# Segment recalls as sixteen packed products behind a block's values, from a dense memory

## Chip, cores and metric

The kernel runs on one core of one Trainium2 chip. The metric is the device time of a run in microseconds (us), as the median of several runs. Most runs of this kernel agree within 0.3%. All arithmetic that decides the output is done on fp32 data; the large products are made of split operands (a high part in the format fp32r and a remainder).

## The reference

One token block goes through a layer norm, and then through two branches whose outputs are added to the input: an attention with a running memory, and a gated feed-forward network. Cut to what matters:

```python
xn = layernorm(x)                        # S = 2048 tokens, D = 448
# attention, H = 16 heads of Dh = 28; 4 segments of L = 512 tokens
phi = lambda t: where(t > 0, t + 1, exp(t))
M, z = 0, 0                              # per head: 28 x 28, and 28
for s in range(4):
    qs, ks, vs = q[s], k[s], v[s]
    a_dot = softmax(qs @ ks.T * scale + causal_mask) @ vs
    num = phi(qs) @ M                    # the recall of a segment
    den = phi(qs) @ z + 1e-6
    o[s] = g * num / den + (1 - g) * a_dot      # g = sigmoid(beta), per head
    M = M + phi(ks).T @ vs               # the update of the memory
    z = z + phi(ks).sum(over tokens)
out = x + o @ wo + (sigmoid(xn @ w_gate) * (xn @ w_up)) @ w_down
```

The first segment's memory is empty, so only three segments have a recall.

## The kernel before

A block is a segment of 512 tokens; there are four (b = 0 to 3). The program has a front and a second phase.

*The front* goes block by block. The order of PE, ACT and DVE in it is the order in which the code is written (`tc.manual_schedule`); SP and POOL get their instructions by a scheduler. For each block, `values(b, t)` multiplies four groups of 128 tokens by the value weights (11 passes of 448 columns each, L335) and puts them into `vst`, where each head takes 32 columns: 28 values, and ones from column 28 on. Then `keys_queries(b, c)` makes seven products of 128 rows (11 passes of 512 columns, L355; c = 0 to 3 hold the keys, 3 to 6 the queries). Each is split on ACT and DVE into two parts that are stored to DRAM (`qd`, L363), and phi of it is made in a tile `e` (ACT: relu and exp; DVE: L365). Phi of queries is stored to `fd` (L368). Phi of keys is turned by four transposes (`key_rows`, L375) and copied by ACT into `kn`, tokens by keys. Between them PE turns the next block's normalised tokens (`turn`, L95; DVE finishes them at L102 and L103), and DVE normalises them (`normalise`, L320).

*The memory* is kept in four tiles `mst` of 112 rows (four heads of 28) and 128 columns (the same four heads' 32 columns of values). `update(b, i)` multiplies `kn` and `vst` for four heads at once, which also gives the products of different heads; a mask `heads` takes these away on DVE (L386, or L389 and L390).

*The recall* of four heads, `recall(b, i, phi)`, is one product of 112 rows with 512 tokens (L401) into a bank "m" or "pd". DVE evaluates it with five instructions: a transpose of 32 by 32 squares into `ts` (L402), three in `weigh` that divide by the ones' column and multiply by the head's gate (L132, L133, L136), and a transpose back into `tb` (L404), which POOL's queue stores to `od` (L405). The recalls of block b - 1 stand in block b for b = 2 and 3: three of them between the values, the fourth behind the first key product. Their four tiles of phi queries (`phi`, 112 rows each, L394) share the five buffers of the tag "e".

*The last block* (b = 3) makes the keys and queries that its own recalls need in another order, c = 3, 4, 5, 6, 0, 1, 2, and begins with the feed-forward network: `next(ffn)` takes one step of the generator `gated`, whose gate products `pgu` (L248) stand between the key products, and whose weights are loaded by SP (`load_up` into `raw`, `load_down` into `rawd`) and split by ACT and DVE (`ready_up`, `ready_down`, L85 and L86). The recalls of block 3 itself stand behind the last two key products and then between gate products. `FILLS` says how many steps of the network come ahead of each of the last two.

*The second phase* runs the network, the attention of 16 units and the output projection against each other; PE's and SP's order there is that of the code. The first scores `st` (L612) stand right behind the gate products at its start.

PSUM's eight banks are shared by tags: two "p", two "s", one "m", two "gu", one "pd". A tile asked of a tag waits until the older one in that bank has been read. In SBUF, `two_k` is a ring of two tiles of 512 columns, which the network's `sg` uses (ACT's tanh L256 writes it, DVE reads it in L257 and L260), and `four_k` one of four pairs (`qk`, `hh`).

```python
def two_k(name):
    return mid.tile([P, L], F32, name=name, tag="2k", bufs=2)
sg = two_k("sg")
A.activation(sg, pgu[0], AF.Tanh, scale=0.5)
V.scalar_tensor_tensor(sg, sg, 1.0, pgu[1], op0=ALU.add, op1=ALU.mult)
```

## Time and profile before

| what | us |
|---|---|
| median of the runs (3; 691.22 to 691.61) | 691.52 |
| the profiled execution's own time | 691.24 |
| its span, first to last instruction | 689.6 |
| the span, by stage: blocks 0 and 1 | 0 to 78 |
| block 2 (the first with recalls) | 78 to 115 |
| block 3, with the network's first steps | 115 to 157 |
| second phase | 157 to 689.6 |

TensorE's granted clock is 1.00 in every stage. PE (TensorE) does the matmuls and transposes, PEld its weight loads, which overlap them; DVE is VectorE, ACT is ScalarE, POOL is GpSimd and SP issues most DMAs. A line such as L401 is a line of the program printed above. PE's records are of 3594 matmuls, of which some are passes of one product: a product of fp32 data is made in two passes, so a recall's row shows "x2".

### The profile page before, as it was taken

To read this page: it belongs to the slowest core of one execution; us is meant where nothing else is said; L and a number is where in the kernel's file an instruction comes from. 1 tells how busy PE (TensorE), PEld (TensorE's weight loads), DVE (VectorE), ACT (ScalarE), POOL (GpSimd) and SP (SyncE) were. 2 spreads that over 40 slices of the span, in tenths; PEclk is the share of its full clock that TensorE was granted. 3 is DMA by queue.
4 is the path that set the end of the run, shared out by engine and by line. 5 is a ranking of instruction groups with operands and counts; after the bars stand their busy time and mean duration, and the time that the engine had idled before them with its cause. 6 is when DMAs were issued, how large, how long until landed. Compare 5 with 4: busy or idle time off the path is not lost.

```text
span 689.6 us, 10445 instructions
## 1 busy us (share of the span) xinstructions
PE 682.4 (99%) x3594; PEld 565.6 (82%) x3594; DVE 569.7 (83%) x994; ACT 342.6 (50%) x563; POOL 146.0 (21%) x349
## 2 busy tenths in 40 slices
PE   8999999999999999999999999999999999999997
PEld 7898888778878787788878878787787878878897
DVE  6765795767889898989898989998889889889863
ACT  5837555343455555544555446455544555446220
POOL 4500020101222122221222223222232322222000
PEclk9999999999999999999999999999999999999999
DMA  7446566696243233333233342324342432333342
GB/s 266 183 146 240 194 224 235 255 331 161 77 102 95 61 86 86 81 112 102 56 71 103 70 123 56 101 55 116 81 114 56 96 72 71 86 95 80 91 155 106
DMA packets 45797, 84.37 MB, mean 122 GB/s; under 512 B 6321, under 2 KB 20401, under 8 KB 45233
## 3 DMA queue, kind: packets, MB, share of 16 engines
q1 hardware_dynamic: 42736, 76.37, 35.9%
q0 software_dynamic: 3008, 7.34, 4.9%
q8 instruction: 28, 0.46, 0.3%
q14 instruction: 25, 0.20, 0.1%
HBM read 51.05 MB, written 32.64 MB: 121 GB/s over the span
## 4 chain that ended last, share of the span: by engine, by line
PE 77%; DVE 10%; issue 7%; POOL 3%; ACT 1%; DMA 1%; SPq 0%; POOLq 0%; ACTq 0%
PE pgu L248 30%; PE pd L173 14%; PE pp L355 10%; PE po L771 5%; PE pv L335 5%; PE st L612 4%; PE pa L687 4%; DVE mx L629 2%; POOL w L627 2%; PE pmm L383 2%; PE n L401 1%; DVE acc L176 1%; DVE w L666 1%; DMA acc<-in_x 1%; PE pt L95 1%
## 5 line engine op out<-in xcount | busy, mean ns | idle before, releaser
L248 PE MATMUL pgu<-xs,wgu 128*128 128x512 f32 x1232 | 316.8, 395 | 0.0
L248 PEld LDWEIGHTS pgu<-xs,wgu 128*128 128x128 f32 x1232 | 226.6, 188 | 45.0 <-issue 3.2
L173 PE MATMUL pd<-wdn,hh 128*128 128x448 f32 x672 | 161.8, 367 | 0.0
L667 ACT ACTIVATE w<-w 128x1024 f32<-128x1024 f32 (+1 forms) x96 | 87.1, 915 | 96.5 <-DVE w L666 95.8
L173 PEld LDWEIGHTS pd<-wdn,hh 128*128 128x128 f32 x672 | 123.0, 188 | 14.5 <-issue 0.6
L627 POOL TENSOR_SCALAR_AFFINE_SELECT w<-w 128x256 f32<-128x256 f32 (+1 forms) x160 | 79.1, 496 | 251.5 <-ACT w L616 216.3
L666 DVE TENSOR_TENSOR w<-w,mb 128x1024 f32<-128x1024 f32 (+1 forms) x96 | 99.7, 1050 | 0.2
L616 ACT ACTIVATE w<-st 128x512 f32<-128x512 f32 x128 | 74.8, 588 | 41.3 <-PE st L612 41.2
L629 DVE TRANSPOSE_TENSOR_REDUCE mx<-w 128x32 f32<-128x1024 f32 x64 | 79.1, 1235 | 12.9 <-POOL w L627 12.8
L355 PE MATMUL pp<-xs,wqk 128*128 128x512 f32 x308 | 77.7, 401 | 0.0
L176 DVE TENSOR_TENSOR acc<-pd,acc 128x448 f32<-128x448 f32 x112 | 67.4, 602 | 2.0 <-PE pd L173 2.0
L355 PEld LDWEIGHTS pp<-xs,wqk 128*128 128x128 f32 x308 | 56.8, 188 | 13.4 <-issue 2.4
L612 PE MATMUL st<-qk 84*128 84x128 f32 (+3 forms) x256 | 64.1, 311 | 0.4 <-ACT w L616 0.3
L259 ACT ACTIVATE hh<-sg 128x512 fp32r<-128x512 f32 x56 | 35.1, 626 | 47.3 <-DVE sg L257 37.3
L612 PEld LDWEIGHTS st<-qk 84*128 84x128 f32 x256 | 48.4, 189 | 9.3 <-ACT w L616 1.9
L256 ACT ACTIVATE sg<-pgu 128x512 f32<-128x512 f32 x56 | 33.2, 593 | 33.4 <-PE pgu L248 32.9
L656 DVE STREAM_TRANSPOSE mb<-top 128x1024 f32<-128x1024 f32 x32 | 39.8, 1243 | 10.3 <-POOL top L653 10.1
L362 DVE TENSOR_TENSOR qk<-pp,qk 128x512 fp32r<-128x512 f32 x28 | 19.3, 688 | 29.8 <-ACT e L360 23.7
L257 DVE SCALAR_TENSOR_TENSOR sg<-sg,pgu 128x512 f32<-128x512 f32 x56 | 37.4, 668 | 4.3 <-PE pgu L248 4.3
L260 DVE SCALAR_TENSOR_TENSOR hh<-sg,hh 128x512 fp32r<-128x512 f32 x56 | 38.4, 685 | 2.4 <-ACT hh L259 2.2
L335 PE MATMUL pv<-wv,xs 128*128 128x448 f32 x176 | 39.8, 376 | 0.2
L687 PE MATMUL pa<-w,vv 128*32 128x128 f32 (+3 forms) x512 | 39.6, 436 | 0.1
(100 smaller groups left out, 637.3 us busy)
## 6 DMA issues: line engine op xcount, KB each, us to landing
qk<-qd SPq DMA_DIRECT2D x192, 112.0 KB
qd<-qk SPq DMA_DIRECT2D x28, 512.0 KB
raw<-in_w_ffn SPq DMA_DIRECT2D x14, 512.0 KB
vd<-vst SPq DMA_DIRECT2D x4, 1024.0 KB
vv<-vd SPq DMA_DIRECT2D x16, 256.0 KB
od<-w POOLq DMA_DIRECT2D x16, 256.0 KB, 3.8
sums<-od SPq DMA_DIRECT2D x32, 128.0 KB
out<-acc SPq DMA_DIRECT2D x16, 224.0 KB
```

The lines of the kernel that those rows point to most:

```text
L173: T.matmul(pd[:, :D], l, r, start=n == 0, stop=n == len(mms) - 1)
L176: V.tensor_add(acc[b][:, t, :], pd[:, :D], acc[b][:, t, :])
L248: T.matmul(dst, wgu[f][:, w, side * P:(side + 1) * P], xs[b][:, a, :], start=n == 0, stop=n == len(TERMS) - 1)
L335: T.matmul(pv[:, :D], xs[b][:, a, t * P:(t + 1) * P], wv[w], start=n == 0, stop=n == len(TERMS) - 1)
L355: T.matmul(pp, wqk[c][:, w, :], xs[b][:, a, :], start=n == 0, stop=n == len(TERMS) - 1)
L612: T.matmul(st[:, at:at + L - kb * P], self.qk[:KS, 1, h, kb * P:(kb + 1) * P], self.qk[:KS, 0, h, kb * P:], start=True, stop=True)
L616: A.activation(w, st, AF.Copy)
L627: G.affine_select(d, d, pattern=pattern, base=0, channel_multiplier=-1, compare_op=ALU.is_ge, fill=MASK)
L629: V.tensor_reduce(mx[:, 16 * (n - 1):16 * (n + 1)], w3[:, n // 2, :2 * L].rearrange("p (b n) -> p b n", n=32), axis=mybir.AxisListType.X, ...
L666: V.tensor_sub(w, w, m)
L667: A.activation(w, w, AF.Exp, scale=SCALE)
L687: T.matmul(pa[32 * j:32 * j + 32, kb * P:], self.vv[:, kb, 32 * j:32 * j + 32], self.pairs[j // 2].block(j % 2, kb), start=kb == 0, stop=k ...
```

## The change

Memory becomes dense: one tile `mst` of 128 rows and 128 columns, whose square of 32 rows (i) and 32 columns (j) is head 4j + i. The update's product has values for weights and keys as moving columns, each head's 28 keys and four further columns (`by_head`; behind `kn`'s last key stand zeros). DVE transposes the result into `dm`, one store for each bank of four heads, and after the fourth takes the squares of each row group from it with one copy or addition each: four for a block. The mask is gone.

A segment's recalls are sixteen products of 28 rows and 32 columns, each at its own position of the array (`tile_position=(32i, 32j)`). Row group i writes bank i; its four column groups fill that bank's 128 rows. They stand in one group: behind all of a block's values for blocks 2 and 3, and for the last block's own behind the last key product and the gate products after it. The evaluation, `recalled`, is apart: the first right behind the products, the other three behind the first, second and third key product, and for the last block's own recalls all four in a row. `ts` now comes from the ring `two_k`, as does `dm`. The gates are also kept by the new order of heads (four more small loads of `beta`). Phi of queries is one tile with a buffer of its own, loaded by four DMAs of 28 rows; `e` has four buffers instead of five. The stores to `od` take every fourth head.

```diff
...
 FRONT = {mybir.EngineType.PE, mybir.EngineType.Activation, mybir.EngineType.DVE}
 FILLS = (2, 2)
 WARM = 10
+EB = 4
+TB = 2
...
         return ps.tile([P, L], F32, name=name, tag=tag, bufs=banks[tag])
-    gate = keep.tile([P, NG], F32, name="gate")
+    gate = keep.tile([P, NG + HG], F32, name="gate")
     gate_n = keep.tile([P, NG], F32, name="gate_n")
...
     with tc.tile_pool(name="front", bufs=2) as sb, tc.manual_schedule(engines=FRONT):
-        heads = sb.tile([P, P], F32, name="heads", bufs=1)
...
-        mst = [[sb.tile([GW, P], F32, name=f"mst{n}_{i}", bufs=1) for i in range(NG)] for n in range(2)]
+        mst = [sb.tile([P, P], F32, name=f"mst{n}", bufs=1) for n in range(2)]
...
             if (c < 4 and b < NB - 1) or (c > 2 and b > 0):
-                e = sb.tile([P, L], F32, name="e", tag="e", bufs=5)
+                e = sb.tile([P, L], F32, name="e", tag="e", bufs=EB)
                 A.activation(e, pp, AF.Relu, scale=-1.0)
                 A.activation(e, e, AF.Exp, scale=-1.0)
             V.tensor_sub(qk[:, 1, :], pp, qk[:, 0, :].bitcast(F32))
...
                     nc.sync.dma_start(fd[b][lo:(c + 1) * P - D], e[D + lo - c * P:])
             return e
+        def by_head(a):
+
+            return bass.AP(a.tensor, a.offset, [list(a.ap[0]), [DH, HG], [1, 32]])
+
         def key_rows(c, e):
             pk = bank("pk", ("m", "pd")[c % 2])
...
             n = min(P, D - c * P)
             A.activation(kn[:, :, c * P:c * P + n], pk.rearrange("p (t n) -> p t n", t=NT)[:, :, :n], AF.Copy)
-        def update(b, i):
-
-            pmm = bank("pmm", ("pd", "m")[i % 2])
+        turned = {}
+
+        def update(b, j):
+
+            if j == 0:
+                turned[b] = two_k("dm").rearrange("p (j n) -> p j n", n=P)
+            dm = turned[b]
+            pmm = bank("pmm", ("pd", "m")[j % 2])
             for t in range(NT):
-                T.matmul(pmm[:GW, :P], kn[:, t, i * GW:(i + 1) * GW], vst[:, t, HG * i:HG * (i + 1), :],
-                         start=t == 0, stop=t == NT - 1)
-            if b == 0:
-                V.tensor_mul(mst[1][i], pmm[:GW, :P], heads[:GW])
-            else:
-                dm = sb.tile([GW, P], F32, name="dm")
-                V.tensor_mul(dm, pmm[:GW, :P], heads[:GW])
-                V.tensor_add(mst[(b + 1) % 2][i], mst[b % 2][i], dm)
-
-        def phi_queries(b, i):
-            phi = sb.tile([GW, L], F32, name="phi", tag="e", bufs=5)
-            nc.sync.dma_start(phi, fd[b][i * GW:(i + 1) * GW])
-            return phi
-
-        def recall(b, i, phi):
-            ts = sb.tile([P, L], F32, name="ts", bufs=1)
-            tb = sb.tile([P, L], F32, name="tb", bufs=2)
-            n2 = bank("n2", ("m", "pd")[i % 2])
-            T.matmul(n2, mst[b % 2][i], phi, start=True, stop=True)
-            V.transpose(ts, n2)
-            weigh(sb, ts, gate[:, i:i + 1], MEM_EPS)
+                keys = by_head(kn[:, t, GW * j:GW * j + HG * 32])
+                T.matmul(pmm[:, :P], vst[:, t, HG * j:HG * (j + 1), :], keys, start=t == 0, stop=t == NT - 1)
+            V.transpose(dm[:, j, :], pmm[:, :P])
+            if j == HG - 1:
+                for i in range(NG):
+                    rows = slice(32 * i, 32 * i + 32)
+                    after, before = (mst[(b + n) % 2][rows, :].rearrange("p (j c) -> p j c", c=32) for n in (1, 0))
+                    if b == 0:
+                        V.tensor_copy(after, dm[rows, :, rows])
+                    else:
+                        V.tensor_add(after, before, dm[rows, :, rows])
+
+        def phi_queries(b, phi):
+            for i in range(HG):
+                nc.sync.dma_start(phi[32 * i:32 * i + DH],
+                                  fd[b].rearrange("(j i d) n -> i d j n", i=HG, d=DH)[i])
+
+        def recall(b, phi, tags):
+
+            n2 = [bank("n2", tag) for tag in tags]
+            for i in range(HG):
+                rows = slice(32 * i, 32 * i + DH)
+                for j in range(NG):
+                    cols = slice(32 * j, 32 * j + 32)
+                    T.matmul(n2[i][cols, :], mst[b % 2][rows, cols], phi[rows, j, :], start=True, stop=True,
+                             tile_position=(32 * i, 32 * j))
+            return n2
+
+        def recalled(b, i, n2):
+            ts = two_k("ts")
+            tb = sb.tile([P, L], F32, name="tb", bufs=TB)
+            V.transpose(ts, n2[i])
+            weigh(sb, ts, gate[:, NG + i:NG + i + 1], MEM_EPS)
             V.transpose(tb, ts)
-            nc.gpsimd.dma_start(od[b][P * i:P * (i + 1)], tb)
+            nc.gpsimd.dma_start(od[b].rearrange("(j i c) n -> i j c n", i=HG, c=32)[i], tb)
...
         with nc.allow_non_contiguous_dma(reason="a strip's heads"):
             for j in range(HG):
-                nc.sync.dma_start(gate[32 * j:32 * j + 32], beta[j::HG].partition_broadcast(32))
+                nc.sync.dma_start(gate[32 * j:32 * j + 32, :NG], beta[j::HG].partition_broadcast(32))
+            for j in range(NG):
+                nc.sync.dma_start(gate[32 * j:32 * j + 32, NG:], beta[HG * j:HG * j + HG].partition_broadcast(32))
...
         split_qk(2)
-        G.memset(heads, 1.0)
-        h3 = heads.rearrange("p (j c) -> p j c", c=32)
-        G.affine_select(h3, h3, pattern=[[-DH, HG], [0, 32]], base=0, channel_multiplier=1,
-                        compare_op=ALU.is_ge, fill=0.0)
-        G.affine_select(h3, h3, pattern=[[DH, HG], [0, 32]], base=DH - 1, channel_multiplier=-1,
-                        compare_op=ALU.is_ge, fill=0.0)
+        G.memset(kn[:, :, D:], 0.0)
         ffn = gated()
         for b in range(NB):
             last = b == NB - 1
-            phi, xn = {}, {}
+            xn = {}
             if b > 1:
-                phi = {i: phi_queries(b - 1, i) for i in range(NG)}
+                phi = sb.tile([P, NG, L], F32, name="phi", bufs=1)
+                phi_queries(b - 1, phi)
             st = None
             for t in range(3 if b == 0 else 0, NT):
                 values(b, t)
-                if b > 1 and t > 0:
-                    recall(b - 1, t - 1, phi[t - 1])
+                if b > 1 and t == NT - 1:
+                    n2 = recall(b - 1, phi, ("gu", "gu", "m", "pd"))
+                    recalled(b - 1, 0, n2)
                 if b == 0:
                     split_qk(t)
                 if last:
...
             e = {}
             for k, c in enumerate((3, 4, 5, 6, 0, 1, 2) if last else range(7)):
                 e[c] = keys_queries(b, c)
+                if b > 1 and k < 3:
+                    recalled(b - 1, k + 1, n2)
                 if b == 0 and c + 4 < 7:
                     split_qk(c + 4)
                 if k == 0:
-                    if b > 1:
-                        recall(b - 1, NG - 1, phi[NG - 1])
                     if b == 0:
                         st = rstd(*st)
...
-                        V.tensor_scalar(gate_n, gate, -1.0, 1.0, op0=ALU.mult, op1=ALU.add)
+                        V.tensor_scalar(gate_n, gate[:, :NG], -1.0, 1.0, op0=ALU.mult, op1=ALU.add)
...
                 if last:
                     if k > 0:
                         next(ffn)
-                    if 2 <= k < 6:
-                        phi[k - 2] = phi_queries(b, k - 2)
+                    if k == 3:
+                        phi = sb.tile([P, NG, L], F32, name="phi", bufs=1)
+                        phi_queries(b, phi)
                     if k > 4:
                         begin[k - 5]()
-                        recall(b, k - 5, phi[k - 5])
                     continue
                 if 2 <= k < 6:
                     key_rows(k - 2, e[k - 2])
...
                         next(ffn)
                     if i == 0:
                         begin[2]()
-                    recall(b, i + 2, phi[i + 2])
+                        n2 = recall(b, phi, ("s", "s", "m", "pd"))
+                    recalled(b, 2 * i, n2)
+                    recalled(b, 2 * i + 1, n2)
```

On PE, in the third block (b = 2; `pv` are values, `n` recalls, `pp` key products, `pt` the next block's tokens, `pk` key rows), this stood before:

```order
L335 MATMUL pv<-wv,xs_67 128x448 x22
L401 MATMUL n_953<-phi,mst_0_126 128x512
L335 MATMUL pv<-wv,xs_67 128x448 x11
L401 MATMUL n_977<-phi,mst_1_127 128x512
L335 MATMUL pv<-wv,xs_67 128x448 x11
L401 MATMUL n_1003<-phi,mst_2_128 128x512
L355 MATMUL pp<-xs_67,wqk_115 128x512 x11
L401 MATMUL n_1045<-phi,mst_3_129 128x512
L355 MATMUL pp<-xs_67,wqk_116 128x512 x11
L95 MATMUL pt<-ident,xn 128x128 x4
L355 MATMUL pp<-xs_67,wqk_117 128x512 x11
L375 MATMUL pk<-ident,e 128x128 x4
```

and this stands now, with the four row groups as four rows of four products:

```order
L336 MATMUL pv<-wv,xs_67 128x448 x44
L417 MATMUL n_973<-phi,mst_122 32x512 x4
L417 MATMUL n_974<-phi,mst_122 32x512 x4
L417 MATMUL n_975<-phi,mst_122 32x512 x4
L417 MATMUL n_976<-phi,mst_122 32x512 x4
L356 MATMUL pp<-xs_67,wqk_114 128x512 x11
L356 MATMUL pp<-xs_67,wqk_115 128x512 x11
L97 MATMUL pt<-ident,xn 128x128 x4
L356 MATMUL pp<-xs_67,wqk_116 128x512 x11
L380 MATMUL pk<-ident,e 128x128 x4
L97 MATMUL pt<-ident,xn 128x128 x4
L356 MATMUL pp<-xs_67,wqk_117 128x512 x11
```

The three recalls between the values and the one behind the first key product have moved into one place ahead of the key products.

On DVE, in the same block, from the end of the normalisation on (`y` is its factor; `qk` and `e` are a key product's two instructions, `ts` to `tb` a recall's evaluation), this stood before, behind three evaluations:

```order
L320 TENSOR_SCALAR xn<-acc_72,mv_925,y_936 128x16x7x4 x2
L362 TENSOR_TENSOR qk<-pp,qk 128x512
L365 SCALAR_TENSOR_TENSOR e<-pp,e 128x512
L402 STREAM_TRANSPOSE ts<-n_1045 128x512
L132 TENSOR_SCALAR rc<-ts 128x16
L133 RECIPROCAL rc<-rc 128x16
L136 SCALAR_TENSOR_TENSOR ts<-ts,gate,rc 128x16x28
L404 STREAM_TRANSPOSE tb<-ts 128x512
L362 TENSOR_TENSOR qk<-pp,qk 128x512
L365 SCALAR_TENSOR_TENSOR e<-pp,e 128x512
L102 TENSOR_TENSOR xs_68<-pt,xs_68 128x3x128
L103 TENSOR_TENSOR xs_68<-pt,xs_68 64x128
```

and this stands now, behind one:

```order
L138 SCALAR_TENSOR_TENSOR ts<-ts,gate,rc 128x16x28
L426 STREAM_TRANSPOSE tb<-ts 128x512
L363 TENSOR_TENSOR qk<-pp,qk 128x512
L366 SCALAR_TENSOR_TENSOR e<-pp,e 128x512
L424 STREAM_TRANSPOSE ts<-n_975 128x512
L134 TENSOR_SCALAR rc<-ts 128x16
L135 RECIPROCAL rc<-rc 128x16
L138 SCALAR_TENSOR_TENSOR ts<-ts,gate,rc 128x16x28
L426 STREAM_TRANSPOSE tb<-ts 128x512
L104 TENSOR_TENSOR xs_68<-pt,xs_68 128x3x128
L105 TENSOR_TENSOR xs_68<-pt,xs_68 64x128
L321 TENSOR_SCALAR xn<-acc_72,mv_919,y_930 128x16x7x4
```

The second of a segment's evaluations has come behind the first key product and the third behind the second, ahead of the next tokens (`xs`).

On SP, in the last block, from the last store of phi queries on (`raw` and `rawd` are the network's weights, `qd` a key product's store, `qk` the attention's first loads), this stood before:

```order
L368 DMA fd_86<-e 128x512
L394 DMA phi<-fd_86 112x512
L363 DMA qd_82<-qk 128x1024
L394 DMA phi<-fd_86 112x512
L363 DMA qd_82<-qk 128x1024
L394 DMA phi<-fd_86 112x512
L192 DMA rawd<-in_w_ffn 128x448
L185 DMA raw<-in_w_ffn 128x1024
L363 DMA qd_82<-qk 128x1024
L595 DMA qk_1642<-qd_79 28x2x512 x6
```

and this stands now:

```order
L369 DMA fd_86<-e 128x512
L364 DMA qd_82<-qk 128x1024
L187 DMA raw<-in_w_ffn 128x1024
L407 DMA phi<-fd_86 28x4x512 x4
L364 DMA qd_82<-qk 128x1024 x2
L194 DMA rawd<-in_w_ffn 128x448
L618 DMA qk_1663<-qd_79 28x2x512 x6
```

The loads of phi queries have come together, ahead of the last two key products' stores, and the load of the down weight `rawd` behind both of them. The load of an up weight into `raw` (L185), which stood ahead of the last store, now stands ahead of the loads of phi.

## The prediction

> **What bounds the kernel now.** The page's first lines come first: how full each engine is.
>
> ```profile
> span 689.6 us, 10445 instructions
> PE 682.4 (99%) x3594; PEld 565.6 (82%) x3594; DVE 569.7 (83%) x994; ACT 342.6 (50%) x563; POOL 146.0 (21%) x349
> ```
>
> PE is busy all the time, but an average over stages doesn't say whether PE waits, so next come the busy times by stage (columns: stretch, its length, then PE, PEld, DVE, ACT and POOL with their counts, clock, DMA share, GB/s) and who waited for whom on PE.
>
> ```profile
> 78.00:115.00 37.00, 37.00 (x195) 31.03 (x194) 29.78 (x69) 20.82 (x38) 3.49 (x8) 1.00 0.60 220
> 115.00:157.00 42.00, 42.00 (x177) 32.95 (x176) 29.37 (x53) 16.84 (x28) 2.70 (x5) 1.00 0.79 277
> 157.00:240.00 83.00, 83.00 (x432) 68.74 (x431) 69.97 (x116) 39.79 (x63) 19.26 (x50) 1.00 0.37 100
> 240.00:640.00 400.00, 399.48 (x2132) 326.20 (x2131) 360.76 (x583) 208.28 (x328) 102.40 (x256) 1.00 0.34 85
> PE warm L442 <- POOL ident masks.py:199: 1.5, 1, 1.5
> PE pt L95 <- DVE xn L320: 1.3, 2, 0.7
> PE st L612 <- ACT w L616: 0.3, 1, 0.3
> ```
>
> From 78 to 640 us PE never idles for more than 0.5 us in all, at full clock. So the rule of this kernel is simple: a microsecond taken off PE's instructions in the front is a microsecond off the span, and a microsecond that PE must newly wait there is one on it, since nothing behind it has slack to take it up. The second thing to see is DVE: 29.78 of 37 us in the third block, 80%, so DVE can't be pushed far before PE waits for it.
>
> **What the change saves on PE.** The chain of waits in order of time (start, length, what) runs through PE alone there; it has a recall (L401), a key product (L355), a transpose (L95), key rows (L375), and the attention product (L687) that already runs four products of 32 columns side by side.
>
> ```profile
> 82.36 0.86 PE n L401 x2
> 88.50 0.86 PE n L401 x2
> 89.36 2.51 PE pp L355 x11
> ...
> 92.73 2.52 PE pp L355 x11
> 95.25 0.44 PE pt L95 x4
> 95.69 2.52 PE pp L355 x11
> 98.21 0.44 PE pk L375 x4
> 201.53 2.29 PE pa L687 x32
> ```
>
> One recall is two passes, 0.86; a segment has four, 3.44. No row shows products in different row groups side by side. The nearest, L687, has 32 passes: 8 each of 512, 384, 256 and 128 columns, four columns' groups at a time. One after the other they would take 8 x 1280 columns x 0.84 ns (0.43 us for 512) = 8.6 us; they take 2.29. So four groups really run at once, and 2.29 is 0.14 over the 2.15 of two passes of 1280 columns, which pays the change of shape. The price of sixteen lies between all at once (0.86 + 0.14 = 1.0) and row groups in turn (4 x 0.86 + 0.14 = 3.6). I take 1.1, near the first: the four of L687 share all rows and still overlap, while row groups share neither rows nor a bank. Saved: 3.44 - 1.1 = 2.34 a segment, **7.0 us** in three. [...]
>
> The memory update keeps four matmuls of 128 columns a group, at the same column count: nothing. On DVE it trades a product and an addition for a transpose and a quarter of four small operations, where DVE idles: nothing. The four added gate loads land long before their use: nothing, or 0.3 us if they delay a load.
>
> **What it costs: DVE's work is moved behind PE's.** Before, a recall stands between values, where DVE has little to do. Now all four stand behind the values, and three of their evaluations fall between the key products, where DVE is full. The third block's DVE timeline has all the prices (start, length):
>
> ```profile
> 91.99 0.13 DVE L308 RECIPROCAL y<-y 128x4 f32<-128x4 f32 x1
> ...
> 93.67 0.68 DVE L362 TENSOR_TENSOR qk<-pp,qk 128x512 fp32r<-128x512 f32 x1
> 94.28 0.68 DVE L365 SCALAR_TENSOR_TENSOR e<-pp,e 128x512 f32<-128x512 f32 x1
> 94.87 0.70 DVE L402 STREAM_TRANSPOSE ts<-n 128x512 f32<-128x512 f32 x1
> ...
> 97.47 0.65 DVE L362 TENSOR_TENSOR qk<-pp,qk 128x512 fp32r<-128x512 f32 x1
> 98.04 0.68 DVE L365 SCALAR_TENSOR_TENSOR e<-pp,e 128x512 f32<-128x512 f32 x1
> 98.64 0.54 DVE L102 TENSOR_TENSOR xs<-pt,xs 128x384 fp32r<-128x384 f32 x1
> ...
> 99.52 0.51 DVE L320 TENSOR_SCALAR xn<-acc,mv,y 128x448 f32<-128x448 f32 x1
> 100.06 0.69 DVE L362 TENSOR_TENSOR qk<-pp,qk 128x512 fp32r<-128x512 f32 x1
> ```
>
> One recall's evaluation, five operations, is 97.47 - 94.87 = 2.6 us, of which its first 0.7 frees the bank. A key product's two are 1.2; the next block's tokens (L102 to L320) 1.4; rstd and two normalised tiles 93.67 - 91.99 = 1.7.
>
> *Third block.* Count from the recalls' start. DVE: first bank full at 1.05, evaluated 3.7, rstd and tiles 5.4, key product 0 to 6.6, second recall 9.2, key product 1 to 10.4, third recall's bank ("m") read at 11.1. PE: recalls 1.1, two key products 5.0, transpose 0.44, the third 2.5: at 9.1 it wants bank "m" for key rows. **It waits 2.0.** From there PE needs 0.44 + 0.44 + 2.5 more, 14.5, and wants bank "pd"; DVE finishes the third recall (1.9), tokens (1.4), product 2 (1.2), reads the last bank (0.7): 16.3. **It waits 1.7**, a little less since the rows overlap. Sum 3.7. DVE then has the gaps it had before, and catches up.
>
> *Last block.* Its key products alternate with gate products, 0.91 us each after the second and third, 0.68 after the fourth:
>
> ```profile
> 128.81 0.86 PE n L401 x2
> 129.67 2.52 PE pp L355 x11
> 132.19 0.91 PE pgu L248 x4
> ...
> 139.67 2.49 PE pp L355 x11
> ...
> 128.85 0.60 ACT L356 ACTIVATE qk<-pp 128x512 fp32r<-128x512 f32 x1 [2.83 <-PE pp L355]
> 129.34 0.59 ACT L360 ACTIVATE e<-pp 128x512 f32<-128x512 f32 x1
> ```
>
> DVE starts 1.1 after a key product ends, behind two of ACT's copies: at 4.9. Four steps of 1.2 with three recalls of 2.6 between them end at 4.9 + 12.6 = 17.5. PE: 1.1 + 5.0 + 0.91 + 2.5 + 0.91 + 2.5 + 0.68 + 2.5 = 16.1, and the next gate product takes the "p" bank that the fourth step frees. **It waits 1.4.**
>
> *Handover.* Count from the end of the last key product (149.85 below). Now the last four evaluations stand in one row on DVE, 10.4 us, ahead of the second gate's product, and they share a ring of two tiles with it: ACT's second tanh (L256) must wait until the third recall is evaluated. Before, that tanh ran as soon as PE had its input:
>
> ```profile
> 149.85 0.68 PE pgu L248 x3
> 156.56 6.60 PE pgu L248 x29
> 152.84 0.56 ACT L85 ACTIVATE wdn<-rawd 128x448 fp32r<-128x448 f32 x1
> 154.82 0.60 ACT L256 ACTIVATE sg<-pgu 128x512 f32<-128x512 f32 x1
> DMA to landing us min/median/max: 2.3/3.3/5.4
> 82.50:84.25 1.75, 1.75 (x8) 1.31 (x7) 1.28 (x5) 0.64 (x2) 0.00 (x0) 1.00 0.72 262
> 277.00:280.50 3.50, 3.50 (x18) 3.02 (x18) 3.43 (x6) 2.36 (x4) 0.49 (x2) 1.00 0.86 197
> ```
>
> PE runs 11 gate products (0.227 us each by the row of 29) 2.5, recalls 1.1, then 36 more 8.2, the first score 0.23: at 12.0 it wants the bank that this tanh reads. DVE can start the four only behind the split of a down weight, whose load SP now issues behind four query loads (896 KB) and the last key store, not ahead of it. If DMAs are free then, key store and weight land by 4.0 and the split ends at 4.6; if the query loads, now of 28 rows each, run at the 197 GB/s of the loads of 28 rows at 277 us (the old ones, of 112 rows, ran at 262 with their start), they are 4.7 us and the split ends at 8.3. Middle: 6.5. Third recall evaluated: 2 x 2.6 + 2.6 later, and its second transpose waits for the store of the first (two tiles): started 2.6 + 0.3 later, landed 5.4 after that by the slowest of the landings above, 8.3, against 7.1 when DVE wants it: 1.2. So tanh ends at 6.5 + 7.8 + 1.2 + 0.6 = 16.1, plus 0.2 for the small gaps: PE **waits 4.3**. Ends: 4.6 with a store of 3.3 gives 13.0, a wait of 1.0; 8.3 with stores two us slower gives 6.5. Then ACT, in order, has two gates' work before it copies the first score: before the third score PE **waits 1.5** (tanh 0.6, DVE 0.7, and some 2.5 of recall and gate on DVE before the next tanh, 0.6, DVE 0.7, ACT 0.6 and 0.6 end 5.5 after the tanh could start, where PE is there at 4.0); at least 0, at most 2.
>
> [...]
>
> **Sum.** -7.0 + 3.7 + 1.4 + 4.3 + 1.5 = **+3.9 us**. The profiled execution took 691.24 (span 689.6 and 1.6 around it): 695.1. It is 0.28 under the median of the runs, 691.52, so the median becomes **695.4**. The forecast's own range: with the handover's low ends -7.0 + 3.4 + 1.2 + 1.0 + 0 = -1.4, with the high ones -7.0 + 4.1 + 1.6 + 6.5 + 2 = +7.2: 690.1 to 698.7 (the bank waits are given 0.3 and 0.2 either way for the gaps between DVE's rows).
>
> **Rivals.** *Row groups in turn.* The sixteen products then save nothing: that the change doesn't do what it says. PE pays 3.6, +0.5 in three; the waits stay (DVE's chain starts from the first bank), but the last wait shrinks by the 2.5 that PE comes later: 0.5 + 3.5 + 1.4 + 1.8 + 1.5 = +8.7, 700.2. For it: no row has two row groups at once. Against: L687's overlap. Chance 0.10.
>
> *The handover isn't late: faster.* If the down weight lands at once and the stores by 3.3 us, and gates wait under 0.5 us in all, PE keeps 7.0 - 3.7 - 1.4 = 1.9 of gain: 689.6. It decides where the second tanh ends before 12 us after the last key product. For it: before, ACT's weight split at 152.84 found its load there. Against: even the low end gives 13.0. Chance 0.08.
>
> *Saving and waits even out*, by the forecast's lower half: within 1.4 us of 691.5, chance 0.10. [...]
>
> **The numbers.** 0.2% is 1.4 us, about what a measurement of this kernel can tell from no change. Forecast, slower by more than that: 0.72, in-turn rival 0.10, so slower 0.82, same 0.10, faster 0.08. The range of 8 in 10, leaving out a tenth at each end: 691.0 to 700.0.
>
> **What the profile of the changed kernel would show.** Sixteen products within 1.3 us (over 3 us: the first rival). PE waiting for DVE's transpose of the recall before key rows, twice, about 2 us each, in the third block; once 1.4 us before a gate product in the last; and once 1 to 6 us for ACT's second tanh. If PE shows no idle time over 1 us between 80 and 170 us, the prediction is wrong in its main step.

## The result, and the profile after

The changed kernel takes 715.4 us (median of 4 runs, 713.65 to 717.83) against 691.5: ratio 1.0347, interval 1.0335 to 1.036. It is slower, as forecast, but by 23.9 us and not by 3.9; the range ended at 700.0.

The profiled execution took 714.98, with a span of 713.2. The page's first lines, then PE's waits (us in all, times, longest), then the busy times by stage:

```profile
span 713.2 us, 10588 instructions
PE 691.7 (97%) x3666; PEld 567.8 (80%) x3666; DVE 571.4 (80%) x998; ACT 342.6 (48%) x563; POOL 146.5 (21%) x347
```

```profile
PE pgu L250 <- ACT sg L258: 6.8, 1, 6.8
PE pgu L250 <- DVE e L366: 3.5, 1, 3.5
PE pk L380 <- DVE ts L424: 3.2, 2, 1.7
PE n L417 <- DMA phi<-fd: 1.7, 2, 1.2
...
PE st L635 <- ACT w L639: 0.5, 2, 0.3
PE pt L97 <- DVE xn L321: 0.2, 1, 0.2
```

```profile
78.00:115.00 37.00, 33.72 (x199) 26.98 (x198) 29.18 (x67) 19.41 (x35) 4.05 (x8) 1.00 0.61 189
115.00:157.00 42.00, 38.41 (x188) 30.42 (x187) 21.77 (x41) 14.32 (x24) 2.70 (x4) 0.92 0.69 224
157.00:240.00 83.00, 74.41 (x360) 57.44 (x359) 58.90 (x97) 32.99 (x52) 15.50 (x36) 0.92 0.42 114
240.00:640.00 400.00, 399.39 (x2155) 325.36 (x2154) 358.94 (x578) 207.66 (x326) 100.37 (x258) 1.00 0.34 86
```

Two things are new. PE waits where it never did, and from 115 to 240 us the granted clock is 0.92. Cut at the places where it changes, it is 0.50 in four stretches and 1.00 elsewhere:

```profile
129.99:133.40 3.41, 3.41 (x9) 2.65 (x9) 0.59 (x1) 0.00 (x0) 0.68 (x1) 0.50 0.36 97
...
150.47:153.88 3.41, 3.41 (x10) 2.63 (x9) 1.08 (x1) 0.00 (x0) 0.00 (x0) 0.50 0.82 259
...
164.12:170.94 6.82, 6.36 (x27) 2.68 (x24) 3.32 (x5) 1.71 (x4) 0.00 (x0) 0.50 0.80 259
...
181.19:188.01 6.82, 3.07 (x7) 2.51 (x8) 4.25 (x8) 1.82 (x3) 0.68 (x1) 0.50 0.28 64
```

PE worked 16.25 us in them, and by the clock half of it is lost: 8.1, an estimate (the key product that the first of them falls into took 4.33 us, one before 2.52). That closes the account of the span's +23.6. PE's idle time grew from 7.2 to 21.5, +14.3: the four new waits (6.8 + 3.5 + 3.2 + 1.7 = 15.2), less 1.1 that the tokens' transposes (`pt`) no longer wait. Its busy time grew by 9.3: 8.1 by the half clock, and about the rest in the first 18 us (16.36 us of work instead of 14.96), where a longer warm-up (its first 20 matmuls take 4.64 us instead of 3.86) fills time in which PE waited for tokens before. It delays nothing: the first values start at 8.85 us, before at 8.89. So the packed products saved nothing. The timeline of PE has them (start, length), first those of blocks 2 and 3, then the last block's:

```profile
86.91 2.35 PE L417 MATMUL n<-phi,mst 28*32 28x512 f32 x32
126.78 2.76 PE L417 MATMUL n<-phi,mst 28*32 28x512 f32 x32
162.31 2.50 PE L417 MATMUL n<-phi,mst 28*32 28x512 f32 x16 [1.22 <-DMA phi<-fd]
165.27 2.94 PE L417 MATMUL n<-phi,mst 28*32 28x512 f32 x16 [0.46 <-DMA phi<-fd]
```

2.3, 2.7 and 5.4 us (less what neighbouring records share) are some 10.4, where four recalls a segment took 3 x 3.44 = 10.3 before. (3.6 us of the last group ran at half clock, so up to 1.8 us are counted in the 8.1 too.) And the stores of `tb`, by the tile's own view, with DVE's wait for them (us, times):

```profile
DMA od<-tb: 7.0, 3
...
DMA to landing us min/median/max: 6.6/7.7/9.3
```

They landed after 7.7 us in the median; before, after 3.3.

### The profile page after: what moved, and what is told of

Read it like the earlier page. It is cut to its first block, busy times and chain, and to the rows that moved or that the text cites. A ratio compares the mean times of both kernels' runs of the same rounds, so it can differ in the third digit from the quotient of the medians.

```text
span 713.2 us, 10588 instructions
## 1 busy us (share of the span) xinstructions
PE 691.7 (97%) x3666; PEld 567.8 (80%) x3666; DVE 571.4 (80%) x998; ACT 342.6 (48%) x563; POOL 146.5 (21%) x347
## 3 DMA queue, kind: packets, MB, share of 16 engines
q0 software_dynamic: 5312, 7.36, 5.5%
## 4 chain that ended last, share of the span: by engine, by line
PE 68%; DVE 12%; issue 12%; DMA 3%; POOL 3%; ACT 2%; SPq 0%; POOLq 0%; ACTq 0%; DVEq 0%
PE pgu L250 27%; PE pd L175 14%; PE pp L356 6%; PE po L794 5%; PE pv L336 4%; PE pa L710 4%; PE st L635 4%; DMA od<-tb 2%; DVE mx L652 2%; POOL w L650 2%; PE pmm L394 1%; DVE acc L178 1%; DVE w L689 1%; DMA acc<-in_x 1%; DVE mx L656 1%
## 5 line engine op out<-in xcount | busy, mean ns | idle before, releaser
L250 PE MATMUL pgu<-xs,wgu 128*128 128x512 f32 x1232 | 318.7, 397 | 10.4 <-ACT sg L258 6.8
L356 PEld LDWEIGHTS pp<-xs,wqk 128*128 128x128 f32 x308 | 58.8, 195 | 13.8 <-issue 1.7
L679 DVE STREAM_TRANSPOSE mb<-top 128x1024 f32<-128x1024 f32 x32 | 39.8, 1242 | 10.3 <-POOL top L676 10.1
L357 ACT ACTIVATE qk<-pp 128x512 fp32r<-128x512 f32 x28 | 16.7, 595 | 45.7 <-PE pp L356 44.8
```

The source lines that it names most:

```text
L250: T.matmul(dst, wgu[f][:, w, side * P:(side + 1) * P], xs[b][:, a, :], start=n == 0, stop=n == len(TERMS) - 1)
L356: T.matmul(pp, wqk[c][:, w, :], xs[b][:, a, :], start=n == 0, stop=n == len(TERMS) - 1)
L679: V.transpose(mb.rearrange("p h (b n) -> p (h b) n", n=32), top.rearrange("p h b -> p (h b)").unsqueeze(2).to_broadcast([P, 32, 32]))
```

## Experiments

All ratios are to the kernel before, run on the same chip.

### The stores

Each recall's store as four stores of 32 whole rows (e1):

```diff
-            nc.gpsimd.dma_start(od[b].rearrange("(j i c) n -> i j c n", i=HG, c=32)[i], tb)
+            for j in range(NG):
+                at = 32 * (HG * j + i)
+                nc.gpsimd.dma_start(od[b][at:at + 32], tb[32 * j:32 * j + 32])
```

> The changed kernel with each recall's store cut into four stores of 32 whole rows. Theory (the store with an outermost dimension of 4 is what is slow, 6.6 to 9.3 us instead of 2.3 to 5.4, and DVE stands still for it with two tiles tb): DVE's waits before tb (7.0 us in all) go below 1, the wait for e before a gate product falls from 3.5 to under 1.5, the one for the second tanh from 6.8 to 2 to 4, and with them two of the four stretches at half clock; 702 to 707 instead of 715. Rival (the stores are late only because the queues are full of loads of phi and queries): stores still land after 6 us or more, and the time stays above 711.

It took 705.9 us (1.0209, 1.0171 to 1.0247). The stores' landings, and PE's waits:

```profile
DMA to landing us min/median/max: 1.9/3.1/6.0
```

```profile
PE pgu L250 <- ACT sg L258: 3.9, 1, 3.9
PE pk L380 <- DVE ts L424: 3.2, 2, 1.7
PE pgu L250 <- DVE e L366: 1.4, 1, 1.4
```

The wait for `e` fell to the 1.4 that the prediction had, the tanh's to 3.9, half clock from 20.5 us to 6.8. Only DVE's own wait missed: 1.9 us, not under 1. The same from the other side: the kernel before with the changed shape (e7).

```diff
-            nc.gpsimd.dma_start(od[b][P * i:P * (i + 1)], tb)
+            nc.gpsimd.dma_start(od[b].rearrange("(j i c) n -> i j c n", i=HG, c=32)[i], tb)
```

> The kernel before, only its recalls' stores take every fourth head as the changed kernel's do (so they go to the wrong heads' rows, with the same bytes and the changed shape 4 x 32 x 512). Theory (the shape alone makes a store slow): stores land after 6.5 to 9 us instead of 2.3 to 5.4, DVE waits before tb 2 us or more each time, and PE waits for it; 694 to 700. Rival (the changed kernel's stores are slow from what runs beside them): they land under 6 us and the time stays within 1.4 us of 691.3.

```profile
DMA od<-tb: 8.0, 4
...
DMA to landing us min/median/max: 6.3/8.3/9.8
```

702.4 us (1.0161, 1.0143 to 1.0179): the store's shape alone costs 11.1 us, more than the 3 to 9 that the theory gave it. Third, the changed kernel with its slow stores, but three tiles `tb` (and three `e`; e12):

```diff
-EB = 4
-TB = 2
+EB = 3
+TB = 3
```

> The changed kernel with three tiles tb instead of two (and three buffers e instead of four, to make room); its stores keep their shape and their 6.6 to 9.3 us. Theory (a slow store costs only by the tile that it holds): DVE's 7.0 us of waits before tb fall under 1.5, PE's wait for e to about 1.4 and for the tanh to 3 to 4.5, two stretches of half clock go: 704 to 709. Rival (slow stores also hold up the other DMAs, phi's loads and the weights): phi and weights stay as late, and the time stays above 711.

708.6 us (1.0253, 1.0223 to 1.0282; only two runs, 706.4 and 710.9). DVE waits for no store, while they land after 7.5. That regains 6.4 us, where the fast stores of e1 regained 9.3: a slow store costs mainly by the tile that it holds. The tanh waited 1.7, less than the 3 to 4.5 expected. But phi was still late (PE waited 2.6 for it), and half clock lasted 10.2 us.

What in the shape makes the store slow stays open. POOL's queue sent 7.36 MB in 5312 packets in the changed kernel, and 7.34 MB in 3008 before.

### What sixteen products cost, and the clock

The products of blocks 2 and 3 behind the first key product (e2), and the same three times over (e3):

```diff
-                if b > 1 and k < 3:
-                    recalled(b - 1, k + 1, n2)
+                if b > 1 and k == 0:
+                    n2 = recall(b - 1, phi, ("m", "pd", "gu", "p"))
+                if b > 1 and k < 3:
+                    recalled(b - 1, k, n2)
+                if b > 1 and k == 2:
+                    recalled(b - 1, 3, n2)
...
-            for i in range(HG):
+            for i in [i for _ in range(REPEAT) for i in range(HG)]:
```

> The changed kernel with the sixteen products of blocks 2 and 3 issued behind the first key product, when phi's loads have landed, into banks m, pd, gu and p, evaluated behind the first, second and twice behind the third key product. Theory (the four row groups run at once, and 2.3 to 2.7 us in the changed kernel was waiting for phi's loads inside the group): 1.0 to 1.3 us a segment, and no half clock behind them in block 3. Rival (row groups in turn, or 32 small products that each cost an issue): 2.2 us or more with phi there. The other waits may move; the time alone decides nothing.

> As the kernel with the late recalls, but with the sixteen products issued three times over (the same values again), so PE is busy with small products alone for some 3 us. Theory (products of 28 rows count little for the clock gate, so a stretch of about 2.7 us of a 3.4 us window is enough for half clock): the clock falls to 0.5 behind at least one of the two groups, whichever fills a window. Rival (the clock falls only where PE has nothing to run): it stays at 1.00 behind both groups, though they last as long as the one of 2.7 us that was followed by half clock.

PE's timeline, e2 first, then e3:

```profile
89.51 1.27 PE L417 MATMUL n<-phi,mst 28*32 28x512 f32 x32
132.74 1.25 PE L417 MATMUL n<-phi,mst 28*32 28x512 f32 x32
```

```profile
132.74 3.41 PE L418 MATMUL n<-phi,mst 28*32 28x512 f32 x96
```

Less the shared 0.07 at each end the group takes 1.1, and three take 3.3: the four row groups run at once, as forecast, once phi is there. e3's 96 products take 3.41 us, as long as the shortest stretch at half clock in the changed kernel, and what stands behind them still has full clock.

```profile
132.73:136.14 3.41, 3.41 (x98) 1.56 (x97) 1.51 (x3) 1.72 (x3) 0.00 (x0) 1.00 0.62 251
136.15:139.55 3.40, 3.40 (x15) 2.83 (x16) 2.37 (x5) 0.65 (x2) 0.59 (x1) 1.00 0.99 310
```

So my theory that small products bring half clock falls: the clock is 1.00 behind both of e3's groups, as its rival had it. That the changed kernel's 2.7 us were followed by half clock is most likely because PE stood still between the row groups, waiting for phi (PEld waited 4.9 us for it, four times), which the records, with modelled ends, show as busy; no view shows PE's idle time there itself. Both kernels are no faster (716.0 and 718.4): the evaluations came later still, and in e2 PE waited 5.4 us for tokens and 4.1 for a bank of the recalls.

### Phi's loads

Sixteen loads of 28 rows and 512 columns, each group of heads as soon as it is stored, on top of e1's stores (e5; in the last block from the second key product on):

```diff
-            for i in range(HG):
-                nc.sync.dma_start(phi[32 * i:32 * i + DH],
-                                  fd[b].rearrange("(j i d) n -> i d j n", i=HG, d=DH)[i])
+            for j in groups:
+                for i in range(HG):
+                    at = DH * (HG * j + i)
+                    nc.sync.dma_start(phi[32 * i:32 * i + DH, j, :], fd[b][at:at + DH])
```

> The kernel with four stores a recall, and phi of queries loaded in sixteen loads of 28 rows and 512 columns, each as soon as the four heads that it belongs to are stored, in the last block from the second key product on, instead of four loads that each need all heads. Theory (the sixteen products stretch to 2.5 us, and to 4.6 in the last block, because phi lands late): 1.3 us or less in all three groups, no wait for phi, the key rows' two waits of 1.5 to 1.7 stay; 699 to 703, against 705.9 with the four stores alone. Rival (the loads are late because the queues are full, or smaller loads and SP's waits for stores delay the key stores instead): the groups stay over 2 us or PE waits elsewhere, and the time stays above 704.

703.1 us (1.017, 1.015 to 1.0191), and PE waits for phi nowhere; the last group, in PE's timeline, with what followed:

```profile
152.96 1.22 PE L418 MATMUL n<-phi,mst 28*32 28x512 f32 x32
154.11 8.45 PE L250 MATMUL pgu<-xs,wgu 128*128 128x512 f32 x36
164.84 0.47 PE L639 MATMUL st<-qk 84*128 84x512 f32 x1 [2.28 <-DVE wgu L88]
172.51 3.78 PE L250 MATMUL pgu<-xs,wgu 128*128 128x512 f32 x8 [7.20 <-ACT sg L258]
```

The theory's numbers held, yet the rival's second half came too. SP waited 5.3 us in all, six times, for phi's stores and issued `rawd`, the down weight, at 153.2; before the change it did so at 147.8. ACT had it at 160.3, and the tanh's wait grew to 7.2:

```profile
153.24 1.12 SPq L194 DMA_DIRECT2D rawd<-in_w_ffn  x1
160.27 0.58 ACT L87 ACTIVATE wdn<-rawd 128x448 fp32r<-128x448 f32 x1 [4.98 <-DMA rawd<-in_w_ffn]
```

So most of what PE saved ahead of the handover, it lost in it: its last recalls ended 6 us earlier than in e1, and the median is 2.8 us less.

### The handover

`ts` in a tile of its own, with three `e` (e4):

```diff
-            ts = two_k("ts")
+            ts = sb.tile([P, L], F32, name="ts", bufs=1)
```

> The changed kernel with ts in a tile of its own instead of the ring that the tanh uses (e has three buffers instead of four, to make room). Theory (the second tanh waits for a ring slot that the third recall holds): PE's 6.8 us wait for sg falls under 1.5, and the half clock from 181 us with it; 706 to 709. Rival (the tanh would be late anyhow, since DVE and ACT stand behind late weights): the wait stays above 4.

714.4 us (1.0332, 1.0302 to 1.0362), not 706 to 709. The tanh no longer waits, as the theory had it, but most of the time is lost a little later, on the bank that is evaluated last:

```profile
PE pd L175 <- DVE ts L424: 5.9, 1, 5.9
```

So the ring is one of several places where DVE's four evaluations hold PE. e8 mends them together (e1's stores, small loads of phi in blocks 2 and 3, POOL's queue for the last block's, `ts` of its own, banks pd, s, s, m); e9 also normalises earlier.

```diff
-                        n2 = recall(b, phi, ("s", "s", "m", "pd"))
+                        n2 = recall(b, phi, ("pd", "s", "s", "m"))
...
+                if t == 2 and b > 0:
+                    st = rstd(*st)
+                    for n in range(2):
+                        xn[n] = normalise(b + 1, n, *st[n])
```

> Four stores a recall and early small loads of phi for blocks 2 and 3; the last block's loads of phi go to POOL's queue, which leaves SP free for the weights (rawd and raw are then issued ahead of the last key store, as before the change); ts has a tile of its own (e three buffers), and the last recalls use banks pd, s, s, m in this order. Theory (the handover's loss is the late weights behind phi's loads and key stores, the shared ring and the bank that is evaluated last, and the half clock that follows): PE's wait for the second tanh is gone or under 1.5 us, no half clock, key rows still wait 3 us in block 2 and a gate product 1.4; that is 691.3 - 6.6 (three segments at 2.2 each) + 3.1 + 1.4 + 0 to 2 = 689 to 692. Rival (DVE's four evaluations in a row are late whatever comes before them): a wait of 4 us or more at the first score or the second gate, half clock behind it, 696 or more.

> As the kernel with the mended handover, and the next block's rstd and first two normalised tiles (1.7 us of DVE's time) moved from behind the values to behind the third values, where DVE is idle. Theory (key rows wait in block 2 because DVE is behind by its whole chain from the recalls on): the two waits for key rows fall from 3.1 to about 1.4 in sum, and the time by as much: 687.5 to 690.5. Rival (the wait comes from one evaluation's place and not from the sum of the chain): it stays near 3.

699.8 (1.012, 1.0105 to 1.0135) and 699.0 (1.0107, 1.009 to 1.0124): far below the changed kernel, but both expectations failed. Tanh and score wait for nothing much, as the theory had it, but phi, now loaded from POOL's queue, lands after 7.5 us in the median, and the loss moves there (e8):

```profile
PE pk L380 <- DVE ts L430: 3.1, 2, 1.7
PE n L423 <- DMA phi<-fd: 3.0, 1, 3.0
```

e9's key rows still wait 3.2 us, as the rival said. Its DVE timeline shows why: DVE sits idle for 1.2 us before the first key product's two instructions, and from 92.0 us until it reads the second bank that key rows want, at 102.3, it has no gap worth naming. So the work that stands behind the first key product sets the wait, and what is moved from ahead of it gains nothing.

### Where the evaluations stand

With e5's stores and loads, the products behind the third values and two evaluations there and two behind the fourth, the last block's one by one at their old places (e6):

```diff
+                if b > 1 and t == 2:
+                    n2 = recall(b - 1, phi, ("gu", "gu", "m", "pd"))
+                if b > 1 and t > 1:
+                    recalled(b - 1, 2 * t - 4, n2)
+                    recalled(b - 1, 2 * t - 3, n2)
```

> The same stores and loads, and the evaluations back at the places that they had before the change: the sixteen products of blocks 2 and 3 behind the third values, two evaluations there and two behind the fourth, ahead of all key products; the last block's products behind the sixth key product and its gate step, the evaluations one by one at the four places of before. Theory (the packed products are worth 2.3 us a segment, and all the loss is DVE's evaluations, the stores and phi's loads, with the half clock that their waits bring): no wait of PE over 1 us, clock 1.00, 684 to 688. Rival (something else of the change costs, as the update's new form or the phi tile): above 690.

713.1 us (1.0312, 1.0295 to 1.0329); this expectation failed. Four evaluations in a row outrun two tiles even with short stores: DVE waited 7.0 us for them, the normalisation stood behind it, PE waited 5.3 for tokens, and in the last block all stores of phi came late (PE waited 6.2 for it). Then other places, on e9 (e10), and e10's last block with e9's block 2 and e5's loads (e11):

```diff
-                if b > 1 and k < 3:
-                    recalled(b - 1, k + 1, n2)
+                if (b, k) in AT:
+                    recalled(b - 1, AT[b, k], n2)
...
+AT = {(2, 0): 2, (2, 1): 3, (3, 0): 1, (3, 4): 2, (3, 5): 3}              # e10
+AT = {(2, 0): 1, (2, 1): 2, (2, 2): 3, (3, 0): 1, (3, 4): 2, (3, 5): 3}   # e11
```

> As the last kernel, with the evaluations at other places: in block 2 one place earlier each (two behind the products, then behind the first and the second key product), in the last block the first two behind the products and the first key product, the other two behind the fifth and sixth, behind all of phi's queries; their banks m and pd are not wanted there before. Theory (a place decides: in block 2 key rows wait for an evaluation that stands behind the second key product's own evaluation, and in the last block three evaluations delay the stores of phi, so its loads, so the last sixteen products and the clock): no wait for key rows over 0.5, none for e, none for phi, no half clock; 691.4 - 6.6 + 0 to 2 = 685 to 687. Rival (DMAs are the bound from 115 to 160 us, whatever DVE does): phi still lands after its place on PE, a wait of over 1 us there with half clock behind it, 691 or more.

> The last kernel's places in the last block, but block 2's evaluations back at the changed kernel's places, and the last block's phi in small loads on SP as in the kernel that first had them. Theory (in the last block, phi's stores now come some 3 us earlier and small loads start with each group of heads, so the last sixteen products find phi there): no wait for phi, no half clock, key rows wait 3.2 in block 2 as before; 689 to 693. Rival (SP, which waits for phi's stores, then issues the weights late): PE waits 3 us or more for the second tanh or the first score; 696 or more.

e10: 698.4 (1.0102, 1.0084 to 1.012). Key rows wait no more, but the tokens normalised behind the evaluations do (3.8 us, with a clock of 0.94 from 85 to 115 us), and phi is late by 2.4 as the rival said. e11: 696.0 (1.0072, 1.0058 to 1.0085): three groups of 1.1 to 1.2 us, no wait for phi, and yet 4.1 us before the first score, as its rival had it, and behind it eight gate products take 3.62 us (2.00 in e15).

### What was left

The banks' order alone, s, s, pd, m (e13), and with block 2's recalls in s, m, gu, pd (e14):

> The last mixed kernel with only the banks of the last block's recalls in another order (s, s, pd, m instead of pd, s, s, m), so that the banks that the first scores want are evaluated first and the one that is wanted last is evaluated last; no instruction changes its place. Theory (the rest of the loss is waits on banks): the wait of 4.1 us before the first score and the half clock behind it (2.4 us) go, but for 0 to 2 us that the next bank then costs; 689.5 to 691.5, against 696.0. Rival (something else of the change costs that much): within 1 us of 696.

> As the kernel with that order, and block 2's recalls in banks s, m, gu, pd instead of gu, gu, m, pd: the bank that the first key rows want is then evaluated one place earlier, and the third recall takes one that is wanted only behind the second key rows. Theory: the two waits for key rows (3.2 us in all) fall to about 1.1, the second alone; 2.1 us under the other kernel of this pair, 687.4 to 689.5, which is under the 691.2 of before. Rival (DVE's chain sets it, wherever the banks are): the first wait only moves to the second, 3 us there.

695.9 (1.0066, 1.0053 to 1.0078) and 697.5 (1.0092, 1.0078 to 1.0106): both theories failed. In the second kernel the keys' wait only moved (3.1 on the second), as it would where DVE's row of work behind the first key product sets it. The score's wait, which e11 and e13 put down to DVE, is named otherwise in e14:

```profile
PE st L640 <- DMA qk<-qd: 4.5, 1, 4.5
PE pk L381 <- DVE ts L426: 3.1, 1, 3.1
```

It is the query loads. (In e13 the DVE instruction that the view names reads bank pd, which a score doesn't want.) A first score needs six of them. In the six runs whose first score waits (e5, e11, e13, e14 and the last two below) it starts 6.2 to 7.4 us after SP is done with issuing the sixth. Before the change it starts 8.0 us after that, at 163.0, without a wait: by these runs PE could have come 0.6 to 1.8 us earlier with the loads issued when they were. In the changed versions they are also issued 2.8 us later and more. Whether the loads land so late because the DMA engines are full (a share of 0.84 to 1.04 from 130 to 165 us, already before the change) was not tested. Last, e13 with the attention five network steps later (e15), the kernel before with the same (e16), and the banks pd, s, s, m with shifts of five (e17_lead20) and three steps (e17_lead18):

```diff
-LEAD, TAIL = 15, 53
+LEAD, TAIL = 20, 53
```

> The kernel with the banks s, s, pd, m, and only the attention's first step put five steps of the network later (LEAD 20 instead of 15: eleven gate products and six down products, 3.8 us, stand ahead of the first score). Theory (query loads that land some 6.5 us after the sixth of them is issued hold the first score, at 164 us, whatever PE has saved before): the wait of 3.8 us and the half clock behind it (1.7 us) go, 690 to 692 against 695.9; if the attention can be shifted at no cost it beats the kernel before, if only just. Rival (another wait takes its place, as the gates' or the down products' for DVE's last evaluations): 694 or more.

> The kernel before with the same LEAD of 20. Its first score waits for nothing now, so the theory expects no gain: within 1.4 us of 691.3, and so the difference between this pair is what packing is worth with the handover out of the way. Rival (the shift itself moves the later stages): more than 1.4 us either way.

> The kernel with the attention five steps later, with the last recalls' banks in the order pd, s, s, m again: the down products want pd first, the scores s some 1.3 us later. Theory (the last bank wait of 1.8 us goes, nothing takes its place): 691 to 691.5, equal to the kernel before and 1.5 under its control with the same shift (692.9). Rival (the first score now waits for s, or the time is set by DMAs whatever the bank): 692.5 or more.

> The same with a shift of three steps instead of five: the first score stands ahead of the six down products, 2.5 us later than without a shift. Theory (query loads allow a first score at 164.5 us, where PE now arrives at 163.2; a smaller shift costs the tail less): a wait of about 1.3 us, no half clock, 690.5 to 692. Rival: a wait of over 2 us with half clock behind it, 693 or more.

692.9 (1.0024, 1.0012 to 1.0036) for e15: 3.0 less than e13, and the profiled execution has a mean clock of 1.0 (four of the nine runs, 694.0 to 694.9, show 0.997). The control e16 takes 692.9 too (1.002, 1.0011 to 1.0028), so the shift itself costs 1.4. With the banks in order and five steps it is 691.8 (1.0015, 1.0003 to 1.0027), with three steps 694.4 (1.0051, 1.0036 to 1.0066; PE waits 2.5 for query loads, as its rival had it, at a mean clock of 0.997). The best packed kernel (its page's line first, then the control's) has 5.1 us less of PE's work, and waits 3.2 more for key rows and 1.0 for query loads:

```profile
PE 678.8 (98%) x3666; PEld 562.4 (82%) x3666; DVE 569.7 (83%) x998; ACT 341.7 (50%) x563; POOL 164.1 (24%) x383
```

```profile
PE 683.9 (99%) x3594; PEld 566.3 (82%) x3594; DVE 568.2 (82%) x994; ACT 341.7 (49%) x563; POOL 148.9 (22%) x349
```

```profile
PE pk L381 <- DVE ts L426: 3.2, 2, 1.7
...
PE st L640 <- DMA qk<-qd: 1.0, 1, 1.0
```

By the median no version beat the kernel before; this one is 0.5 us behind it. But its twelve runs range from 690.7 to 695.4 us, those of the kernel before from 691.17 to 691.42: four of the twelve were faster than the median of before, and those over 693.3 show a granted clock of 0.995 to 0.998. So half clock probably follows a wait in some of its executions and not in others.

## Why the prediction was right and wrong

- **Saving of 7.0: nothing came.** The price of sixteen products, 1.1, was right (1.07 to 1.2 in e2, e5, e11). The step that failed is the one that takes phi to be there when they start. Each row group now takes heads from all of phi, so no load can start before the last store of phi has landed; the prediction costed the loads' rows, not their start. The groups so took 2.3, 2.7 and 5.4 us. SP's wait, and in the last block the last store of phi and the loads:

```profile
SPq L407 <- DMA fd<-e: 7.1, 3, 2.5
```

```profile
149.85 0.55 SPq L369 DMA_DIRECT2D fd<-e  x1
...
159.00 1.64 SPq L407 DMA_DIRECT2D phi<-fd  x4
```

- **Third block 3.7:** measured 3.2, in two waits. Right, and it stays in every version that keeps these places.
- **Last block 1.4:** right in size and place (1.4 in e1 and e5). In the changed kernel it was 3.5, the rest a store.
- **Handover 4.3 + 1.5:** measured 6.8 + 0.5. The ring was the place, though without it the last bank takes its part (e4). Two terms were mis-sized. The store, "landed 5.4 after that", was 6.6 to 9.3; DVE waited 3.6 us for it and not 1.2. The down weight's split was to end 4.6 to 8.3 us after the last key product; ACT's began 12.8 after it:

```profile
171.41 0.58 ACT L87 ACTIVATE wdn<-rawd 128x448 fp32r<-128x448 f32 x1 [4.07 <-DMA rawd<-in_w_ffn]
```

- **The store's shape:** The sum has no term for it, and no row of before shows the two us by which the high end's stores are slower. The changed kernel's landed 4.4 us later in the median (7.7 against 3.3), e7's 5.0 (8.3), and e1's, of whole rows, after 3.1.
- **No term for the clock: at most 8.1.** Every wait was priced at its own length. The profiled executions with a single wait of 2.3 us or more on PE's view (the changed kernel, e1 to e14 and e17_lead18) have mean clocks of 0.981 to 0.998, those without one (before, e15, e16 and e17_lead20) 0.999 or 1.0. In e15 waits of 1.8 and 1.7 us stand at a mean clock of 1.0. A stretch of 3.41 us at half clock cost the key product in it 1.8 us (4.33 against 2.52).
- **The bound behind PE:** "a microsecond taken off PE's instructions in the front is a microsecond off the span" is wrong beyond the 0.6 to 1.8 us that the query loads leave, an estimate from when the first scores started.
- **Sums that do not come out.** The high end of the second tanh's wait is 8.3 + 7.8 + 3.2 + 0.6 + 0.2 - 12.0 = 8.1 by its own terms, not 6.5; the pieces listed for the third score add up to 6.3, not 5.5. Mended, both would raise the forecast's range, but not to 23.9.

The measured terms in the prediction's order, 0 + 3.2 + 3.5 + 6.8 + 0.5, and 1.7 for phi and 8.1 for the clock, make 23.8 against the span's 23.6; that is closer than the terms are known, as 1.8 of them may be counted twice. That the change came out slower, as forecast, rests on the waits, which were named in the right places; the size does not follow from the forecast's sum. The rival of row groups in turn fell with e2 and e3: once phi is there, they run at once. The one that the handover isn't late fell as well, and the one that saving and waits even out.

## What to carry to other kernels

When work on a full engine is packed or moved, ask first when its operands land: a group that starts together starts with its last load. Two spare tiles hid stores that landed after 3.3 us, and not those of 7.7, so look at the shape of each store that an edit touches, and price a wait on PE with the half clock that may follow it. Then look for the next transfer that PE will meet earlier than before.

## What the hardware showed

In the changed kernel the four stretches at half clock last 3.41, 3.41, 6.82 and 6.82 us and begin 20.48, 13.65 and 17.07 us apart, which is 6, 4 and 5 times 3.41. Ahead of the second and the last of them PE stood idle for 2.82 of 3.40 us (from 147.06) and 3.06 of 3.40 (from 177.78). The nearest cases: idle 1.70 of 3.39 (e7), no change; idle 1.94 of 3.39 (e6), half clock. e15's longest wait, 1.77 us, stands at a mean clock of 1.0. First e7, then e6:

```profile
174.71:178.10 3.39, 1.69 (x8) 1.47 (x9) 1.74 (x3) 2.58 (x5) 0.24 (x1) 1.00 0.48 135
178.12:181.50 3.38, 3.38 (x18) 2.96 (x17) 2.28 (x4) 0.00 (x0) 1.31 (x4) 1.00 0.25 42
```

```profile
93.41:96.80 3.39, 1.45 (x7) 0.87 (x5) 1.21 (x2) 2.42 (x5) 0.31 (x2) 1.00 0.56 198
96.82:100.22 3.40, 0.03 (x1) 0.04 (x1) 3.05 (x11) 0.00 (x0) 2.80 (x7) 0.50 0.34 77
```

The other two stretches of the changed kernel stand behind less recorded idle time: 0.04 of 3.40 us (from 126.58) and 1.32 of 3.40 (from 160.71). Both times hold a group of sixteen products that came in pieces as phi landed, where busy records are no proof of work.
